# Loading input tiles 10 to 15 later in the DMA queue of a linear-attention and MLP kernel

## The chip, the cores and the metric

The kernel runs on one core of a Trainium2 chip. TensorE (PE) multiplies matrices, VectorE (DVE) and ScalarE (ACT) work element by element and read PE's results from its accumulation banks, GpSimd (POOL) takes part of the same kind of work, and SyncE (SP) issues nearly all DMAs, one after the other. The metric is the time of one execution in microseconds (us); less is better.

## The reference

The input x has 2048 tokens of 512 features. One layer norm is shared by two branches, and the result is x + A(xn) + B(xn):

```python
xn = _layernorm(x)                                   # over the 512 features
# A: linear attention, 32 heads of 16
q, k, v = heads of xn @ wqkv                         # wqkv is 512 x 1536
pq, pk = phi(q), phi(k)                              # phi(t) = (t + 1 if t > 0 else exp(t)) + 1e-6
kv = sum over tokens of pk^T v ; z = sum over tokens of pk
A = (pq @ kv / (pq . z + 1e-6)) @ wo
# B: MLP with a squared relu, 1376 hidden features
B = relu(xn @ w1 + b1)**2 @ w2 + b2
```

The sums kv and z run over all tokens, so they have to be finished before any token's attention can be.

## The kernel before

The 2048 tokens are 16 tiles of 128 (numbered 0 to 15). Float32 products are made of parts: each operand is split into a high part, which PE can take exactly, and the low rest, and three products of parts stand for one.

The program has two halves. The first, up to about 90 us, walks over the tiles and sums `kx`, the products of the keys' features and the normalised tokens. The second, to the end, makes queries, MLP and attention output for four blocks of four tiles. The change lies in the first half.

The program is ordered by hand: every engine executes its instructions in the order in which the Python code issues them, and waits for the inputs of each. SP's queue of DMAs is such an order too: a DMA that has to wait for its source holds up those behind it.

What one tile i passes through in the first half:

- `load_x` (L157) loads raw tokens from DRAM. Tiles 0 to 3 come alone, 4 to 7 in one DMA into `x4`, and 8 to 11 in one DMA into `x8`, each of 1 MB; 12 and 13, and 14 and 15, come in two DMAs of 512 KB each.
- `measure` (L230) takes mean and variance on VectorE (`bn_stats`, `bn_aggr`); `roots` makes the reciprocal root, mainly on POOL; `normalise` (L248) writes the normalised tile `xp`, for tiles from 5 on with ScalarE.
- The tile is needed with the features in the partitions as well. Tiles 0 to 2 are turned by PE. From tile 3 on, `regroup` (L277) stores the tile to DRAM (`via<-xp`, one DMA; for tiles from 6 on one for a pair), `move` (L286) fetches it back in four DMAs (`xg<-via`, `xg4s` for tiles 3 to 5), and `turn` (L291) transposes 32x32 blocks on VectorE. `regroup` puts the moves on a list; `move()` issues what is on it. The moves wait for the store to have landed.
- `transposed` (L314) splits the turned tile into high and low part (ScalarE, then VectorE), and `keep_t` stores the turned tile of the first eight to DRAM for the second half (`xTd<-t`).
- `project` (L373) multiplies with the keys' weights (12 matmuls, `pk`), `phi_k` and `parts` make the features and their parts (ScalarE and VectorE), and `kx` (L390) sums the products with the tokens (12 matmuls).

The loop over steps i from 2 to 15 (L812) starts with `move()`. Then PE does `project(i)` and, at the end of the step, `kx(i - 1)`: 24 matmuls, which take about 5.4 us. In step 3 and later steps up to 10, at the end, the columns of tile i + 2 are turned and split and another `move()` is called (L886 and L887), after which one tile's statistics are measured (L894): tile 10 in step 4, 11 in step 5, 12 in step 6, and so on to 15 in step 9. Tiles 8 and 9 are measured in step 3 (L874).

Before the loop, tile 3 is normalised and stored, and then stand these lines (L645 to L647):

```python
    normalise(*fourth)      # tile 3; its store is issued in here
    load_x(8, x8)
    move()                  # the four moves of tile 3
```

Of the kernel before, what the change touches and what calls it, by code (L numbers as in the profile page):

```python
# [18 lines left out]
def kernel(  # L19
# [59 lines left out]
    def bank(name, tag="ps"):  # L79
        return psum.tile([P, 512], F32, name=name, tag=tag)  # L80
# [6 lines left out]
    def next_tag(of):  # L87
        k, n = turns[of]
        turns[of][0] = (k + 1) % n
        return f"{of}{k}"  # L90

    def two(name):
        return keep.tile([P, 2, 512], F32, name=name, tag=next_tag("x"))

    def four(name, tag, dt=F32, pool=None):
        return (pool or work).tile([P, TB, 512], dt, name=name, tag=tag)
# [60 lines left out]
    def load_x(i, t):  # L157
        n = t.shape[1]
        nc.sync.dma_start(t, xf[i * P:(i + n) * P, :].rearrange("(i p) d -> p i d", i=n))
        for k in range(n):  # L160
            xr[i + k] = t[:, k]
# [11 lines left out]
    def units(f):  # L173


        if f < NF - 1:
            return [(0, f * P, P)]
        return [(0, f * P + Q, 2 * Q), (2 * Q, f * P, Q), (3 * Q, f * P, Q)]
# [10 lines left out]
    def load_o():  # L189
        o = wos[0] = four("wo", "ra")  # L190
        for j in range(NJ):
            cut = P - Q * j
            for a, z, to in ((0, cut, Q * j), (cut, P, 0)):
                if z > a:
                    nc.sync.dma_start(o[to:to + z - a, j], wo[j * P + a:j * P + z, :])
# [34 lines left out]
    def measure(g, *ks):  # L230

        tiles, st, mv, _ = g
        for k in ks or range(len(tiles)):
            nc.vector.bn_stats(st[:, k, :], xr[tiles[k]])  # L234
            nc.vector.bn_aggr(mv[:, k, :], st[:, k, :])
# [6 lines left out]
    def roots(tiles, st, mv, y):  # L242

        n = len(tiles)
        (nc.vector if tiles[0] in (0, 1, 6) else nc.gpsimd).tensor_scalar(y[:, 1, :n], mv[:, :n, 1], 1e-5, None, op0=OP.add)
        nc.gpsimd.tensor_tensor(out=y[:, 0, :n], in0=y[:, 1, :n], in1=power[:, :n], op=OP.pow)

    def normalise(tiles, st, mv, y):  # L248

        n = len(tiles)  # L250
        r, u = (y[:, k, :n] for k in range(2))
        if tiles[-1] >= NACT:

            nc.vector.scalar_tensor_tensor(u, mv[:, :n, 0], -1.0, r, op0=OP.mult, op1=OP.mult)
        later = []

        def last(i, o, src, k):
            nc.scalar.activation(o, src, AF.Identity, bias=u[:, k:k + 1], scale=r[:, k:k + 1])
            if i in groups:
                regroup(i)  # L260

        for k, i in enumerate(tiles):
            o, src = xp[i], xr[i]
            if i >= NDVE:

                o, src = o.rearrange("p g (j c) -> p g j c", j=NJ), gjc(src)
            if i < NACT:
                nc.vector.tensor_scalar(o, src, mv[:, k, 0:1], r[:, k:k + 1], op0=OP.subtract, op1=OP.mult)
                if i in groups:
                    regroup(i)  # L270
            else:
                later.append(lambda a=(i, o, src, k): last(*a))
        return later
# [12 lines left out]
    def move(n=8):  # L286
        for _ in range(n):
            if moves:
                nc.sync.dma_start(*moves.pop(0))
# [22 lines left out]
    def transposed(i, n=1):  # L312

        b, at = i // TB, slot(i)  # L314
        if i < NDVE:
            t = turned_pe(i, n)
        else:
            t = [xT[b][:, :, at] if i >= NPE else w512(f"t{i}", "p", 6).rearrange("p (j t) -> p j t", j=NJ)]
            turn(t[0], xg[i])
        m = NJ // n  # L320
        h, l = ([x[:, k * m:(k + 1) * m, at] for k in range(n)] for x in cols(i))

        def high(k=0):
            nc.scalar.activation(h[k], t[k], AF.Copy)  # L324

        def low(k=0):
            nc.vector.tensor_tensor(out=l[k], in0=t[k], in1=f32(h[k]), op=OP.subtract)

        def keep_t():
            o = t[0]  # L330
            if i < NDVE:
                o = w512(f"t{i}", "p", 6).rearrange("p (j t) -> p j t", j=NJ)
                for k in range(n):
                    copy("act", o[:, k * m:(k + 1) * m], t[k])
            if i < NPE:
                nc.sync.dma_start(xTd[b][:, :, at], o)

        return high, low, keep_t

    def run(*what):  # L340
        for f in what:
            f()
# [30 lines left out]
    def project(i, ps, w, steps, first=True, last=True):  # L373

        for n, (j, u, v) in enumerate(steps):
            nc.tensor.matmul(ps, lhsT=cols(i)[u][:, j, slot(i)], rhs=w[v][:, j, :], start=first and n == 0,  # L376
                             stop=last and n == len(steps) - 1)
# [174 lines left out]
    x4, x8 = four("x4", "r1"), four("x8", "r2")  # L552
    for i0 in range(0, NT, TB):
# [6 lines left out]
        if i0 < NPE:  # L560
            single = work.tile([P, 3, 512], F32, name=f"xg{i0}s", tag="r0")
            for k in range(3):
                i = i0 + k - 1
# [3 lines left out]
        for k in range(0, n, 2):  # L567
            i = i0 + TB - n + k
# [74 lines left out]
    keep1()  # L643
    rests_k("dve", 3)
    normalise(*fourth)  # L645
    load_x(8, x8)
    move()  # L647
    high, low, keep2 = transposed(2)
    high()
# [20 lines left out]
    def tokens_sum(n, tag):  # L670
        return keep.tile([P, 2, 2, 512], F32R, name=f"T{n}", tag=tag)
# [32 lines left out]
    def fetch():  # L704
        while todo and len(held) < 3:
            held.append(todo.pop(0)())
# [95 lines left out]
    def more(i=None):  # L802

        if i is None or i > 12:
            do(extra, counts[0].pop(0))
# [6 lines left out]
    for i in range(2, NT):  # L812
        if i == 13:
            nc.sync.dma_start(b1s[:, :NF - 1], b1[:(NF - 1) * P].rearrange("(f p) -> p f", p=P))
            for a, o, n in units(NF - 1):
                nc.sync.dma_start(b1s[a:a + n, NF - 1:], b1[o:o + n, None])
        move()
        if i in (4, 6):
            load_x(i + 8, two(f"x{i + 8}"))
        if i == 9:  # L820
            load_o()
        if i > 10:
            fetch()
        ps = pks[i] if i < 3 else bank(f"pk{i}")
        if i > 2:
            project(i, ps, wk, HL)
        high = low = keep_t = lambda: None
        if i <= NDVE:
            high, low, keep_t = transposed(i + 1)
        if i == 2:  # L830
            measure(soon)
            roots(*soon)
        later = normalise(*soon) if i == 3 else []

        soon_turned = transposed(i + 2) if 11 <= i and i + 2 < NT else ()

        def mid():
            if i != 3:
                high()
            more(i)  # L840

        def late():
            if i == 3:
                high()
                run(*later)
                tokens(3)
            low()
            more(i)

        if i == 12:  # L850
            rawz = raw_1(NF - 1)
            T.update({n: tokens_sum(n, f"B{n - 1}") for n in (1, 2)})
        if i == 12:
            w = load_1("q", 0)
        if i == 13:
            todo_1 = operands_first(0, w)
            extra.append(todo_1.pop(1))
        if i == 14:
            z = pair("w1z0")
            extra.append(lambda: split(z[:, 0], z[:, 1], rawz, "act", "dve"))  # L860
            o34 = halves(four("Tf", "r0"))
            extra.extend(sums_of(xT[NB - 1], xT[NB - 2], *o34))
            lows = [extra.pop() for k in range(2)]
            extra += [todo_1[0], lows[1], todo_1[1], lows[0], *todo_1[2:]]
        phi_k(i, ps, mid, late)
        more(i)
        run(*soon_turned)
        if i != 3:
            later = normalise(*soon) if soon else []
        if i == 2:  # L870
            ahead[3] = group(6, 7)
            measure(ahead[3], 0)
        if i == 3:
            measure(ahead[4])  # L874
        parts(i)
        if i == 2:
            tokens(2, ahead=False)
            run(*later)
            later = []
        keep_t()  # L880
        if 2 < i < NT - 1:
            tokens(i + 1)
        if i != 3:
            run(*later)
        if NDVE < i + 1 < 12:
            high, low, keep_t = transposed(i + 2)  # L886
            run(high, low, move, keep_t)  # L887
        pieces(int(i > 11))
        if i == 2:
            measure(ahead[3], 1)  # L890
        if i + 2 in (4, 6, 8, 10):
            ahead[i + 2] = group(i + 6, i + 7)
        if 3 < i < 10:
            measure(ahead[(i + 2) // 2 * 2], i % 2)  # L894
        soon = ahead.get(i + 1, ())
        if soon:
            roots(*soon)
        kx(i - 1)
        more(i)
# [66 lines left out]
    for n in range(2):  # L966
# [306 lines left out]
        f = NF - 2  # L1273
# [125 lines left out]
```

## Time and profile before

| | us |
|---|---|
| Time, median of 3 runs | 410.56 |
| lowest and highest run | 410.22 and 410.93 |
| The profiled execution's own time | 410.95 |
| its span in the trace | 409.2 |
| TensorE busy | 402.3 |
| VectorE busy | 308.9 |
| ScalarE busy | 267.6 |
| GpSimd busy | 50.4 |

The span reaches from the first to the last recorded instruction; the rest of the profiled execution's time lies around it. L12 in a row means line 12 of the kernel, and a helper's line stands for all its calls. A row of instructions has its start, its length, the engine, the line, the operation, output and input, and, in brackets, how long the engine had been idle and what ended the idle time. A row of waits has the waiting instruction, what it waited for, and the total, the count and the longest of the waits. A row of windows has, for a stretch of time, its length, the busy time of PE, of PE's weight loads, of VectorE, ScalarE and GpSimd, then the granted clock, the share of the DMA engines in use and the GB/s that they moved.

### The profile page before, as it was taken

To read this page: it belongs to the slowest core of one execution; us is meant where nothing else is said; L and a number is where in the kernel's file an instruction comes from. 1 tells how busy PE (TensorE), PEld (TensorE's weight loads), DVE (VectorE), ACT (ScalarE), POOL (GpSimd) and SP (SyncE) were. 2 spreads that over 40 slices of the span, in tenths; PEclk is the share of its full clock that TensorE was granted. 3 is DMA by queue.
4 is the path that set the end of the run, shared out by engine and by line. 5 is a ranking of instruction groups with operands and counts; after the bars stand their busy time and mean duration, and the time that the engine had idled before them with its cause. 6 is when DMAs were issued, how large, how long until landed. Compare 5 with 4: busy or idle time off the path is not lost.

```text
span 409.2 us, 5634 instructions
## 1 busy us (share of the span) xinstructions
PE 402.3 (98%) x1939; PEld 330.5 (81%) x1939; DVE 308.9 (75%) x560; ACT 267.6 (65%) x465; POOL 50.4 (12%) x81
## 2 busy tenths in 40 slices
PE   8989999999999999999999999999999999999996
PEld 6868888888788888888878888888888888878885
DVE  6877666597898999988349997567989676449833
ACT  4667667556888789887728751677587856837520
POOL 6435333220000000030000300000000200001200
PEclk9999999999999999999999999999999999999999
DMA  6937636820332231272564912411121790034612
GB/s 214 320 121 266 209 104 206 240 45 0 101 109 79 77 103 27 95 198 42 189 229 139 209 34 100 118 53 51 51 79 40 227 197 26 0 108 150 105 26 103
DMA packets 46735, 49.00 MB, mean 120 GB/s; under 512 B 8242, under 2 KB 31026, under 8 KB 46451
## 3 DMA queue, kind: packets, MB, share of 16 engines
q1 hardware_dynamic: 44402, 44.46, 35.1%
q0 software_dynamic: 2304, 4.20, 6.5%
q8 instruction: 15, 0.25, 0.2%
q14 instruction: 14, 0.11, 0.1%
HBM read 37.76 MB, written 9.70 MB: 116 GB/s over the span
## 4 chain that ended last, share of the span: by engine, by line
PE 94%; DMA 2%; DVE 2%; ACT 0%; SPq 0%; issue 0%
PE acc L131 37%; PE b L495 33%; PE kx L396 9%; PE pk L376 9%; PE acc L506 2%; PE pz L131 1%; DMA xg4s<-via 1%; DMA via<-xp 1%; PE b L131 1%; PE pz0b L131 1%; DVE st L234 1%; DMA x<-in_A_x_dram 1%; DVE wkl L581 0%; ACT xs1h L324 0%; PE acc L513 0%; PE pkv L933 0%
## 5 line engine op out<-in xcount | busy, mean ns | idle before, releaser
L131 PE MATMUL acc<-w2r,s 128*128 128x512 f32 x477 | 112.8, 390 | 0.0
L131 PEld LDWEIGHTS acc<-w2r,s 128*128 128x128 f32 x477 | 89.4, 188 | 19.3 <-issue 0.7
L495 PE MATMUL b<-T,aop 128*128 128x512 f32 x336 | 83.4, 389 | 0.0
L495 PEld LDWEIGHTS b<-T,aop 128*128 128x128 f32 x336 | 63.0, 188 | 13.9 <-ACT t L112 0.8
L1071 POOL DMA_DIRECT2D res<-in_B_b_dram x16 | 14.4, 1100 | 276.8 <-DVE dt L437 91.4
L396 PE MATMUL kx<-pk,tok 128*128 128x512 f32 x192 | 46.0, 389 | 0.0
L396 PEld LDWEIGHTS kx<-pk,tok 128*128 128x128 f32 x192 | 36.0, 188 | 7.6
L495 PE MATMUL b<-xs0h,aop 128*128 128x512 f32 x112 | 36.9, 390 | 0.0
L131 PE MATMUL acc<-mh,aTsr 128*128 128x512 f32 x112 | 35.6, 389 | 0.0
L1079 DVE TENSOR_TENSOR res<-acc,res 128x512 f32<-128x512 f32 x16 | 10.7, 689 | 20.4 <-PE acc L131 19.0
L112 ACT ACTIVATE aop<-S 128x512 fp32r<-128x512 f32 x28 | 17.5, 624 | 12.6 <-DVE S L733 12.6
L357 POOL TENSOR_TENSOR tok<-xp,tok 128x512 fp32r<-128x512 f32 x15 | 20.1, 1342 | 39.1 <-ACT tok L112 39.1
L495 PEld LDWEIGHTS b<-xs0h,aop 128*128 128x128 f32 x112 | 21.0, 188 | 4.4
L131 PEld LDWEIGHTS acc<-mh,aTsr 128*128 128x128 f32 x112 | 21.0, 188 | 4.3
L123 DVE TENSOR_TENSOR w2r<-r,w2r 128x512 fp32r<-128x512 f32 (+2 forms) x35 | 23.8, 681 | 0.5 <-ACT w2r L112 0.4
L120 DVE TENSOR_TENSOR aop<-S,aop 128x512 fp32r<-128x512 f32 x28 | 19.2, 687 | 4.8 <-ACT aop L112 4.4
L120 DVE TENSOR_TENSOR s<-c,s 128x512 fp32r<-128x512 f32 x20 | 13.6, 689 | 11.4 <-ACT s L112 11.3
L495 PE MATMUL b<-xs0l,aop 128*128 128x512 f32 x56 | 21.8, 389 | 0.0
L131 PE MATMUL acc<-ml,aTsr 128*128 128x512 f32 x56 | 21.8, 389 | 0.0
L112 ACT ACTIVATE w2r<-r 128x512 fp32r<-128x512 f32 x32 | 19.6, 619 | 2.1 <-DMA out_dram<-res 2.0
L495 PE MATMUL b<-xs1h,aop 128*128 128x512 f32 x56 | 19.5, 389 | 0.0
L112 ACT ACTIVATE T<-Tf 128x512 fp32r<-128x512 f32 x16 | 9.5, 624 | 14.4 <-DVE Tf L676 14.3
(196 smaller groups left out, 751.9 us busy)
## 6 DMA issues: line engine op xcount, KB each, us to landing
r<-in_B_w_dram SPq DMA_DIRECT2D x49, 256.0 KB, 3.1
res<-in_A_x_dram SPq DMA_DIRECT2D x8, 512.0 KB, 4.2
res<-in_B_b_dram POOLq DMA_DIRECT2D x16, 256.0 KB, 5.7
out_dram<-res SPq DMA_DIRECT2D x15, 256.0 KB, 2.1
via<-xp SPq DMA_DIRECT2D x5, 512.0 KB, 2.8
xg<-via SPq DMA_DIRECT2D x20, 128.0 KB, 2.6
x<-in_A_x_dram SPq DMA_DIRECT2D x2, 1024.0 KB, 6.5
xTd<-t SPq DMA_DIRECT2D x8, 256.0 KB, 3.0
```

The source lines that it names most:

```text
L112: nc.scalar.activation(o, i, AF.Copy, bias=bias)
L120: ENG[el].tensor_tensor(out=l, in0=src, in1=f32(h), op=OP.subtract)
L123: nc.vector.tensor_tensor(out=l, in0=src, in1=f32(h), op=OP.subtract)
L131: nc.tensor.matmul(ps, lhsT=a[u], rhs=b[v], start=first and n == 0, stop=last and n == 2)
L234: nc.vector.bn_stats(st[:, k, :], xr[tiles[k]])
L357: ENG[el].tensor_tensor(out=l, in0=src, in1=f32(h), op=OP.subtract)
L376: nc.tensor.matmul(ps, lhsT=cols(i)[u][:, j, slot(i)], rhs=w[v][:, j, :], start=first and n == 0, stop=last and n == len(steps) - 1)
L396: nc.tensor.matmul(kxp[c], lhsT=tok[i][:, u, c * P:(c + 1) * P], rhs=pk[i][:, v], start=i == 0 and (u, v) == first, stop=i == NT - 1 and ( ...
L495: nc.tensor.matmul(ps, lhsT=a[u][:, j * P:(j + 1) * P], rhs=b[v][:, j, :], start=first and j == 0 and n == 0, stop=last and j == 1 and n == 2,
L506: nc.tensor.matmul(ps, lhsT=s[u][:, k * P:(k + 1) * P], rhs=w2s[NF - 1][u][:, a:z], start=first and u == 0, stop=stop and u == 1)
L1071: nc.gpsimd.dma_start(r[:, i], b2[None, :].partition_broadcast(P), accum_op=OP.add)
L1079: nc.vector.tensor_tensor(out=r[:, a:z], in0=ps, in1=r[:, a:z], op=OP.add)
```

## The change

The load of tiles 8 to 11 in front of tile 3's moves becomes a load of tiles 8 and 9 alone, into the first half of the same buffer. Tiles 10 and 11 are loaded into its second half at the start of step 4, where tiles 12 and 13 were loaded; these go to step 5, and tiles 14 and 15 from step 6 to step 7. All loads remain on SP's queue, and the buffers of tiles 12 to 15 are the same.

```diff
@@ -643,7 +643,7 @@
     keep1()
     rests_k("dve", 3)
     normalise(*fourth)
-    load_x(8, x8)
+    load_x(8, x8[:, :2])
     move()
     high, low, keep2 = transposed(2)
     high()
@@ -815,8 +815,10 @@
             for a, o, n in units(NF - 1):
                 nc.sync.dma_start(b1s[a:a + n, NF - 1:], b1[o:o + n, None])
         move()
-        if i in (4, 6):
-            load_x(i + 8, two(f"x{i + 8}"))
+        if i == 4:
+            load_x(10, x8[:, 2:])
+        if i in (5, 7):
+            load_x(i + 7, two(f"x{i + 7}"))
         if i == 9:
             load_o()
         if i > 10:
```

## The prediction

> **What bounds the kernel now.** First the page: the shares of the span and the granted clock.
>
> ```profile
> span 409.2 us, 5634 instructions
> PE 402.3 (98%) x1939; PEld 330.5 (81%) x1939; DVE 308.9 (75%) x560; ACT 267.6 (65%) x465; POOL 50.4 (12%) x81
> PEclk9999999999999999999999999999999999999999
> ```
>
> TensorE (PE) is busy for 402.3 of 409.2 us at full granted clock, so a change can win only from the other 6.9 us. Second, where those lie: the windows, then the waits of PE.
>
> ```profile
> 0.00:24.00 24.00, 20.58 (x97) 16.64 (x98) 16.79 (x37) 12.75 (x25) 11.19 (x29) 1.00 0.77 245
> 24.00:404.00 380.00, 380.00 (x1833) 312.38 (x1832) 290.54 (x522) 254.88 (x440) 39.20 (x53) 1.00 0.39 111
> PE pk L376 <- ACT xs1h L324: 1.8, 2, 1.6
> ```
>
> From 24 to 404 us PE never stops. Before 24 us it stands for 24.00 - 20.58 = 3.42 us, and 1.6 us of that is one wait, on the transposed columns of a token tile. What was late there is in the chain of waits (start, us, what):
>
> ```profile
> 13.05 2.77 DMA via<-xp
> ...
> 15.84 0.33 SPq L289
> ...
> 17.16 4.79 DMA xg4s<-via
> ...
> 21.98 0.72 DVE t L293
> ...
> 22.72 0.64 ACT xs1h L324
> ...
> 23.40 3.02 PE pk L376 x12
> ```
>
> This is tile 3: stored to DRAM, fetched back by four moves, turned by VectorE, split by ScalarE, projected by PE. The last move, 64 KB, took 4.79 us, to 21.95. The DMA issues, looked at in short windows (KB each, us from issue to landing), say how unusual that is; the rows are, in order, the fourth move of tile 3 with its neighbour, two moves of tile 4, the load of tiles 8 to 11, and the loads of tiles 12/13 and 14/15:
>
> ```profile
> xg4s<-via SPq DMA_DIRECT2D x2, 64.0 KB, 4.9
> xg4s<-via SPq DMA_DIRECT2D x2, 64.0 KB, 1.9
> x<-in_A_x_dram SPq DMA_DIRECT2D x1, 1024.0 KB, 7.8
> x<-in_A_x_dram SPq DMA_DIRECT2D x1, 512.0 KB, 5.2
> x<-in_A_x_dram SPq DMA_DIRECT2D x1, 512.0 KB, 4.1
> ```
>
> SP's queue, in order of time:
>
> ```profile
> 13.45 0.43 SPq L159 DMA_DIRECT2D x<-in_A_x_dram  x1
> 15.84 1.76 SPq L289 DMA_DIRECT2D xg4s<-via  x4
> 18.39 0.34 SPq L281 DMA_DIRECT2D via<-xp  x1
> ...
> 33.50 1.73 SPq L289 DMA_DIRECT2D xg<-via  x4
> 35.32 0.52 SPq L336 DMA_DIRECT2D xTd<-t  x1
> 35.89 0.63 SPq L159 DMA_DIRECT2D x<-in_A_x_dram  x1
> 38.51 0.34 SPq L281 DMA_DIRECT2D via<-xp  x1
> 42.41 1.74 SPq L289 DMA_DIRECT2D xg<-via  x4
> 44.24 1.21 SPq L336 DMA_DIRECT2D xTd<-t  x2
> 45.50 0.65 SPq L159 DMA_DIRECT2D x<-in_A_x_dram  x1
> ```
>
> The 1 MB load (13.45) is queued ahead of the moves (15.84) and lands at 13.45 + 7.8 = 21.25; the moves land just behind it, at 21.95. So the load delays tile 3, and with it PE.
>
> **Part 1: half of that load goes.** 512 KB fewer lie ahead of the moves. The soonest that the last move can then land is 17.16 + 1.9 = 19.06. The latest: between 16.0 and 18.4 the queues moved 338 GB/s (the next fence); if the landing moves up only by what 524,288 bytes take at 400 GB/s (an estimate above that rate, so a smaller gain), 1.3 us, it is 20.65. I take a value near the soonest, because by 18.4 us 2.4 x 338 = 811 KB had passed after 16.0, and half a load plus four moves is 524 + 262 = 786 KB: the moves would be through before the next store (18.39) joins.
>
> ```profile
> 16.00:18.40 2.40, 2.40 (x12) 1.99 (x11) 2.23 (x4) 2.13 (x4) 1.70 (x4) 1.00 0.93 338
> 19.17 0.68 DVE L357 TENSOR_TENSOR tok<-xp,tok 128x512 fp32r<-128x512 f32 x1
> 23.40 0.50 PE L376 MATMUL pk<-wkh,xs1h 128*128 128x512 f32 x1 [1.62 <-ACT xs1h L324]
> ```
>
> VectorE works on tile 1's low part until 19.17 + 0.68 = 19.85, so the turn of tile 3 starts at about 19.86 in place of 21.98: **VectorE and ScalarE gain 2.12 us**. PE follows the turn by 23.40 - 21.98 = 1.42 us, so it could start at 21.28; its own earlier matmuls end at 23.40 - 1.62 = 21.78. **PE gains the whole 1.62 us**, and is then bound by itself. At the other bound (20.65) both gain 1.3 us. A loss has no mechanism here: bytes only leave the queue. What is late next, tile 4's turn, hangs on a store at 18.39 that now meets fewer bytes too.
>
> **Part 2: tiles 10 and 11 are loaded in step 4**, where tiles 12 and 13 were: same place in SP's queue (behind the moves of 33.50 and the store of 35.32), same 512 KB. So the 35.89 row prices it: issued at 35.89, landed 5.2 later, 41.09 on the old clock. But tile 10 has a reader in that same step: its statistics on VectorE.
>
> ```profile
> 39.83 0.69 DVE L234 BATCH_NORM_STATS2 st<-x 128x6 f32<-128x512 f32 x1
> 40.55 0.18 DVE L235 BATCH_NORM_AGGREGATE mv<-st 128x2 f32<-128x6 f32 x1
> 40.65 0.66 DVE L371 SCALAR_TENSOR_TENSOR k<-pk,k 128x512 f32<-128x512 f32 x1
> 41.34 0.63 ACT L112 ACTIVATE pk<-k 128x512 fp32r<-128x512 f32 x1 [1.00 <-DVE k L371]
> 42.64 2.88 PE L396 MATMUL kx<-pk,tok 128*128 128x512 f32 x12
> 49.89 0.69 DVE L234 BATCH_NORM_STATS2 st<-x 128x6 f32<-128x512 f32 x1
> 59.95 0.69 DVE L234 BATCH_NORM_STATS2 st<-x 128x6 f32<-128x512 f32 x1
> ```
>
> The statistics start 39.83 - 35.89 = 3.94 us after the issue; the data come after 5.2. **New wait: 1.26 us on VectorE**, whatever the common shift, since the issue hangs on the same chain (tile 5's normalisation, stores, moves) that follows tile 3's turn. Queued behind it on VectorE is the feature map of step 5 (40.65), for it ScalarE's rounding of the keys (41.34), for that the key products on PE (42.64). The rounding ends at 41.97, 0.67 us before PE wants it; with the wait it ends at 43.23. All this is on the old clock. With VectorE's gain it ends at 43.23 - 2.12 = 41.11, while PE, 1.62 earlier, wants it at 41.02: **PE loses about 0.1 us**. In general the net gain is the smaller of 1.62 and VectorE's gain less 0.59. By the bounds of part 1 (2.12 and 1.3) that is 1.53 and 0.71. If the load takes only 4.1 us, as the later one of the same size did, the wait is 0.16 and nothing is lost. ScalarE's further work of that step is also late, but the next key products come 5.4 us later, and VectorE has pauses on the way (1.00 in the 41.34 row).
>
> The Trainium skill, in "DMA: Bandwidth & Descriptors", section "Anatomy of one DMA", fits a transfer as 2.0 us and its bytes at 436 GB/s. By that fit, an estimate, 512 KB take 3.2 us, the data are there before the statistics ask, and part 2 costs nothing. The trace disagrees: 5.2 and 4.1 us for that size, so the rows decide. The same page's "Rules for kernel authors" ask for 1 MiB or more in a DMA, which speaks against cutting the load; by its fit the cut costs another 2.0 us, though only where somebody waits for it.
>
> **Part 3: tiles 12/13 in step 5, 14/15 in step 7.** SP then issues the first between the two stores of the 44.24 row, at 44.24 + 1.21/2 = 44.85, and it lands after 4.1 to 5.2 us, at 48.95 to 50.05; its reader is at 49.89. At worst 0.16 us late, against a slack like the 0.67 above: nothing. The second comes behind the moves of tiles 10 and 11 (issued 51.66 for 1.75):
>
> ```profile
> 51.66 1.75 SPq L289 DMA_DIRECT2D xg<-via  x4
> 58.81 0.34 SPq L281 DMA_DIRECT2D via<-xp  x1
> ```
>
> So it is issued at 53.4 and lands by 58.6, its reader is at 59.95, and the next store at 58.81: nothing. SP issues one DMA more in all, about 0.63 us (35.89 row), ahead of a store of turned columns that only the second half of the program reads: nothing. POOL's queue is not touched.
>
> **Sum.** -1.62 (gap) + 0.1 (new wait on PE) = -1.5 us. The profiled execution took 410.95 us for a span of 409.2; that gives a span near 407.7 and 409.45. It lies 0.39 above the median of 410.56; on the median the forecast is **409.05 us**. No change can be told from a measurement within 0.2%, 0.82 us.
>
> **Rivals.** (a) *The moves gain little.* The bytes that came behind (the store of 18.39) may have shared the engines, so that the landing moves up only by 1.3 us; the net is then 0.71, 409.85. For it: no row shows in which order the engines served the queued bytes. Against: 786 KB fit in before 18.4.
> (b) *No wait at all in step 4*: the load comes within 4.1 us, 1.62 stays, 408.95. For it: the 45.50 row. Against: the 35.89 row is the one at this place, with the same moves before it and the store of 38.51 behind it. The page's fit, above, would give this result.
> (c) *Slower: the load of tiles 10 and 11 is so late that PE stands longer than before.* Place: the key products at 42.64. PE loses there what it won when issue (35.89 - 2.12 = 33.77) + landing + 2.14 (39.83 to 41.97) passes 42.64, which is a landing of 6.7 us; at 7.5 it is 0.8 slower. The 1 MB load took 7.8: with that the time is 33.77 + 7.8 + 2.14 - 42.64 = 1.07 longer, 411.65. Or the issue does not move up, because ScalarE or SP was bound by something else: 35.89 + 5.2 + 2.14 - 42.64 = 0.59 slower. Against: 7.8 is for twice the bytes, and each row between tile 3's turn and the issue is queued behind it.
> (d) *The gap stays* because another input of tile 3's turn is late: 410.55. Against: VectorE is free at 19.85, and the chain of waits puts only the move ahead of the turn.
>
> **Chances.** The forecast 0.62; (a) 0.14, half of it beyond the 0.82 us bound; (b) 0.09; (c) 0.10; (d) 0.05. Faster: 0.62 + 0.09 + 0.07 = 0.78; same: 0.05 + 0.07 = 0.12; slower 0.10. The range goes from (b) less 0.37 us, the reach of the runs from their median, to (a) with the same on top: 408.6 to 410.2. (c) and (d) lie outside. Alone, the forecast's own range is 408.7 to 409.5.
>
> **What would show it.** Right: the moves of tile 3 land before 20 us; PE's wait on the split columns in front of tile 3's projection is under 0.2 us; the load of tile 10 is issued near 33.8 and VectorE's statistics wait on it for about 1.3 us; PE's key products of step 5 wait for ScalarE by 0.1 to 0.3; from then on PE stands nowhere, and its busy time stays 402.3. Wrong: a landing of the moves after 20.7, an issue of tile 10's load near 35.9, a landing over 6 us, or new waits of PE after 60 us, which would mean that the later loads matter.

## The result and the profile after

The changed kernel takes 409.23 us (median; 409.01 to 410.12), the kernel before 410.56 (410.22 to 411.18): a ratio of 0.997, 95% interval 0.9958 to 0.9982, all of it below 1. That is 1.33 us less; 409.05 was forecast. The profiled execution took 410.11 us, with a span of 408.4; among the runs of the changed kernel that is one of the longest, for a reason that lies in its first microseconds and is told below.

The page of the changed kernel (first two lines), its waits of PE and its windows:

```profile
span 408.4 us, 5632 instructions
PE 403.4 (99%) x1939; PEld 331.8 (81%) x1939; DVE 308.4 (76%) x560; ACT 267.7 (66%) x465; POOL 49.8 (12%) x81
...
PE warm L526 <- PEq L1387: 0.8, 1, 0.8
PE pk L376 <- DVE wkh L116: 0.6, 1, 0.6
...
0.00:24.00 24.00, 22.51 (x101) 18.52 (x102) 17.64 (x39) 13.24 (x26) 11.34 (x30) 1.00 0.68 224
24.00:404.00 380.00, 380.00 (x1834) 312.51 (x1833) 289.49 (x520) 254.43 (x440) 38.46 (x51) 1.00 0.40 113
```

PE's wait on tile 3's split columns is gone from the list, and its busy time before 24 us has grown from 20.58 to 22.51 us. The new 0.6 us wait stands at the very start, on the keys' weights. The DMA issues of the weights, looked at in the same short window (2.0 to 2.3 us), first before, then after:

```profile
rk<-in_A_wqkv_dram SPq DMA_DIRECT2D x2, 256.0 KB, 3.8
```

```profile
rk<-in_A_wqkv_dram SPq DMA_DIRECT2D x2, 256.0 KB, 5.4
```

Nothing of the change lies ahead of these loads. They landed 1.6 us later in this execution, and PE's first key products started at 17.11 in place of 16.16. So 1 us of what the change won is hidden in the two profiled executions by an unequal start.

SP's queue, the landing times of the half load, of a move of tile 3 and of the load of tiles 10/11, and VectorE's rows:

```profile
14.63 0.43 SPq L159 DMA_DIRECT2D x<-in_A_x_dram  x1
16.52 1.76 SPq L289 DMA_DIRECT2D xg4s<-via  x4
...
34.74 0.63 SPq L159 DMA_DIRECT2D x<-in_A_x_dram  x1
...
x<-in_A_x_dram SPq DMA_DIRECT2D x1, 512.0 KB, 3.5
xg4s<-via SPq DMA_DIRECT2D x1, 64.0 KB, 1.9
x<-in_A_x_dram SPq DMA_DIRECT2D x1, 512.0 KB, 4.7
...
20.18 0.68 DVE L357 TENSOR_TENSOR tok<-xp,tok 128x512 fp32r<-128x512 f32 x1
20.78 0.70 DVE L293 STREAM_TRANSPOSE t<-xg4s 128x512 f32<-128x512 f32 x1
...
39.51 0.70 DVE L234 BATCH_NORM_STATS2 st<-x 128x6 f32<-128x512 f32 x1 [0.74 <-DMA x<-in_A_x_dram]
```

The last move of tile 3 lands 1.9 us after its issue in place of 4.9; the turn (20.78) follows VectorE's work on tile 1 (20.18) without a wait. In step 4 VectorE stands 0.74 us for tiles 10 and 11. The chain of waits shows what PE makes of it (start, us, what):

```profile
17.27 5.51 PE kx L396 x24
22.78 2.72 PE pk L376 x12
...
39.10 2.72 PE pk L376 x12
41.82 2.92 PE kx L396 x12
44.74 2.72 PE pk L376 x12
```

Twelve matmuls take 2.72 us when nothing disturbs them. Tile 3's projection takes that now, 3.02 before; the key products of tile 5 (the row of 41.82) take 2.92. These are the ones that the prediction and the expectations call the key products of step 5; PE makes them in step 6, between the projections of tiles 6 and 7.

### The profile page after: what moved, and what is told of

Same layout as the page of the kernel before. It is cut to its first block, busy times and chain, and to the rows that moved or that the text cites. A ratio compares the mean times of both kernels' runs of the same rounds, so it can differ in the third digit from the quotient of the medians.

```text
span 408.4 us, 5632 instructions
## 1 busy us (share of the span) xinstructions
PE 403.4 (99%) x1939; PEld 331.8 (81%) x1939; DVE 308.4 (76%) x560; ACT 267.7 (66%) x465; POOL 49.8 (12%) x81
## 4 chain that ended last, share of the span: by engine, by line
PE 97%; DMA 1%; DVE 0%; SPq 0%; issue 0%
PE acc L131 37%; PE b L495 33%; PE pk L376 11%; PE kx L396 11%; PE acc L506 2%; PE pz L131 1%; DMA rk<-in_A_wqkv_dram 1%; PE b L131 1%; PE pz0b L131 1%; PE acc L513 0%; PE pkv L935 0%; PE pm L952 0%; PE pt L308 0%; SPq L159 0%; PE end L131 0%; PE end L506 0%
```

## The experiments

Because starts differ, each profiled execution is read by one account: the start of the first key products (timeline), and the time from there to the projection of step 7 (its start in the chain), less 27.44 us, which is the least that any execution showed for that stretch but for 0.05. The difference is what PE lost in steps 2 to 6. The executions of e7 and e8, in which the granted clock fell, are read apart, further down.

| execution | start | step 7 | loss | its time | time less start and loss |
|---|---|---|---|---|---|
| before | 16.16 | 45.52 | 1.92 | 410.95 | 392.87 |
| changed, first | 17.11 | 44.74 | 0.19 | 410.11 | 392.81 |
| e1, changed | 16.30 | 44.31 | 0.57 | 409.60 | 392.73 |
| e9, changed | 16.43 | 44.16 | 0.29 | 409.48 | 392.76 |
| e2, 1 MB ahead | 16.41 | 45.16 | 1.31 | 410.51 | 392.79 |
| e3, 512 KB before, 512 KB behind the moves | 16.52 | 44.61 | 0.65 | 409.99 | 392.82 |
| e4, all behind the moves | 16.54 | 44.26 | 0.28 | 409.66 | 392.84 |
| e11, 768 KB ahead | 16.43 | 44.27 | 0.40 | 409.59 | 392.76 |
| e6, loads in step 2 | 16.73 | 45.09 | 0.92 | 410.46 | 392.81 |
| e5, late statistics | 16.73 | 44.17 | 0.00 | 409.60 | 392.87 |
| e10, late statistics | 16.51 | 43.90 | -0.05 | 409.27 | 392.81 |

The last column varies by 0.14 us: start and loss account for all differences among these executions, and nothing after step 7 has any part in them.

**The changed kernel again.** No edit.

> The changed kernel once more, as the measure for the other runs of this chip. Theory (bytes): the gap in front of tile 3's projection was the time that the second half of the 1 MB load took ahead of tile 3's moves; it is closed, and VectorE's new wait on the load of tiles 10 and 11 costs PE 0.1 to 0.3 us. Expected: 1.2 to 1.6 us less than before, about 409.1. Rival (later loads): the gain comes from where the loads of tiles 12 to 15 now stand and not from the bytes ahead of tile 3's moves. It expects the same time here; the next two runs tell the two apart.

Measured 409.77 us, ratio to before 0.9971 (0.9961 to 0.9982); 1.30 us less by the medians. Losses of 0.19, 0.57 and, in e9, 0.29 against 1.92.

**Only the rest of the change, the bytes ahead of the moves back.**

```diff
-    load_x(8, x8[:, :2])
+    load_x(8, x8)
     move()
```

> The whole 1 MB load is again ahead of tile 3's moves; all else is as in the changed kernel, so that tiles 10 and 11 are loaded a second time in step 4 and their statistics wait for that. Bytes: the gap of about 1.6 us is back, PE has no lead, and VectorE's wait of 0.7 to 1.3 us exceeds the 0.67 us of slack by 0.1 to 0.6 us: 410.6 to 411.2 us, not faster than before. Later loads: the gain stays, about 409.2 us.

Measured 411.55 us, ratio 1.0019 (1.0004 to 1.0035). Its chain, and then the landing of the second load of tiles 10 and 11:

```profile
17.96 3.62 DMA xg4s<-via
...
23.03 3.06 PE pk L376 x12
...
x<-in_A_x_dram SPq DMA_DIRECT2D x1, 512.0 KB, 4.0
```

The gap is back (a loss of 1.31), with all later loads where the change has them. So the rival, that their places make the gain, falls. The gap is smaller than in the first profile since the last move took 3.62 us and not 4.79; it varies from one execution to the next. In the profiled execution the load of step 4 landed after 4.0 us, just in time, and PE lost nothing there, less than expected. Half of the runs were at 411.9 to 413.7 us, the longest of them at a mean granted clock of 0.996; what PE lost in those was not traced and stays open.

**Only half of the load ahead, all else as early as before** (an edit of the kernel before).

```diff
-    load_x(8, x8)
+    load_x(8, x8[:, :2])
     move()
+    load_x(10, x8[:, 2:])
```

> Only half of the load is ahead of tile 3's moves, the other half (tiles 10 and 11) follows right behind these moves, and tiles 12 to 15 are loaded in steps 4 and 6 as before. Bytes: the gap is closed and nobody waits in step 4: about 409.0 us, 0.1 to 0.3 us under the changed kernel. Tile 4's store has as many bytes ahead of it as before and lands near 22.3 us; its turn may wait by up to 0.3 us, which PE does not feel. Later loads: 410.5 us, as before.

Measured 410.59 us, ratio 0.9992 (0.9983 to 1.0002): not the expected 409.0. Tile 3's gap is closed, but the next fetch pays, in its chain:

```profile
18.78 4.35 DMA via<-xp
...
24.45 1.99 DMA xg4s<-via
...
26.57 0.71 DVE t L293
...
28.00 3.01 PE pk L376 x12
```

Tile 4's store (18.78) now follows the second half and takes 4.35 us, where it took 2.0 us in the changed kernel; its turn and with it the projection of step 4 come late, a loss of 0.65 in all. The bytes had only been passed to the next in the queue. That the change moved tiles 10 and 11 past the store of tile 4 is, by this run, a part of its gain. The runs' median lies 0.6 us above the profiled execution; that rest was not traced.

**Nothing ahead of tile 3's moves.**

```diff
-    load_x(8, x8[:, :2])
     move()
+    load_x(8, x8[:, :2])
```

> As the changed kernel, but the load of tiles 8 and 9 too stands behind tile 3's moves. Bytes, as in the prediction: the moves land as soon as they can, under 2.0 us after the last issue, but VectorE is at work until then and PE is its own bound already, so that the time is that of the changed kernel within 0.3 us. If the half that was left still delayed tile 3, the time falls by over 0.4 us.

Measured 410.16 us, ratio 0.9979 (0.9968 to 0.9989), 0.4 over the changed kernel of the same call. There is no gain, as expected; by the loss (0.28) it is the changed kernel's equal, by the medians 0.1 beyond the expected 0.3. And it shows the same shift as in e3 on a smaller scale: tile 4's turn waits 0.4 us for its moves, and the projection of step 4 takes 2.99.

```profile
DVE t L293 <- DMA xg4s<-via: 0.4, 1, 0.4
...
27.63 2.99 PE pk L376 x12
```

**No wait in step 4.**

```diff
-        if 3 < i < 10:
+        if i == 5:
+            measure(ahead[6])
+        if 5 < i < 10:
             measure(ahead[(i + 2) // 2 * 2], i % 2)
```

> As the changed kernel, but the statistics of tile 10 are taken at the end of step 5, together with those of tile 11, so that no instruction of VectorE in step 4 waits for the load of tiles 10 and 11. Theory (bytes, with a small price for the wait): PE's wait in front of the key products of step 5 is gone, 0.2 to 0.5 us under the changed kernel, 1.5 to 2.1 us under before. Rival (the wait is covered): the statistics waited in PE's slack only, and the time is that of the changed kernel, 1.2 to 1.4 us under before; the two statistics at the end of step 5 then cost as much as they save.

> The changed kernel beside the next two on one chip. From the traces so far, the time of a profiled execution is the start of the first key products on PE, plus what PE loses from there to the projection of step 7 against 27.44 us of pure matmuls, plus 392.8 us. In the changed kernel the loss was 0.2 and 0.6 us, in the kernel before 1.9. Expected: a loss of 0.2 to 0.6 us, 1.2 to 1.6 us under before.

> The changed kernel with the statistics of tile 10 taken in step 5. If its loss is nothing once more, it is 0.2 to 0.6 us under the changed kernel in the same call, and 1.6 to 2.1 us under before. If the earlier difference to the changed kernel came only from the two calls having run on different chips or starts, the two are equal within 0.2 us.

The late statistics measured 409.20 us (0.9958 of before, 0.9945 to 0.9972) and, beside the changed kernel on one chip, 409.13 (0.994, 0.9918 to 0.9962) against 409.57 (0.9951, 0.9931 to 0.997): 0.44 us less by the medians. Against the kernel before it is 2.01 and 1.89 us less by the medians, which agrees with the loss of 1.92 us in the one trace of that kernel. The key products of tile 5 with their neighbours, first in the changed kernel (e9), then with late statistics (e10):

```profile
41.12 0.01 issue
41.13 3.02 PE kx L396 x12
44.16 2.72 PE pk L376 x12
```

```profile
38.46 2.72 PE pk L376 x12
41.18 2.72 PE kx L396 x12
43.90 2.72 PE pk L376 x12
```

So the wait on the load of tiles 10 and 11 does reach PE, and costs 0.2 to 0.6 us in the changed kernel. The late statistics are the fastest version found; PE has no pause left between the first key products and the end.

**The loads of tiles 8 and 9 in step 2** (with late statistics).

```diff
-    load_x(8, x8[:, :2])
     move()
...
         move()
+        if i == 2:
+            load_x(8, x8[:, :2])
```

> As the run before, and the load of tiles 8 and 9 is issued in step 2 behind the moves of tile 4, so that no load lies ahead of the moves of tile 3 or of the store of tile 4. Theory (bytes): neither the projection of tile 3 nor that of tile 4 waits, and nobody waits in step 5: PE runs from its first key products on without a pause, 1.7 to 2.2 us under before. If the load in step 2 delays the store of tile 5 behind it, VectorE's turn of tile 5 waits and some 0.3 us are given back. Rival: the changed kernel has taken what there was, and this is 1.2 to 1.4 us under before.

Measured 410.09 us (0.9974, 0.996 to 0.9988), worse than with the load at its place. What was noted as a risk decides: the store of tile 5 behind the load takes 3.48 us (2.08 in e1), the moves of tiles 6 and 7 are late in turn, and the projection of step 6 is slow to start:

```profile
25.01 3.48 DMA via<-xp
...
34.44 3.25 DMA xg<-via
...
39.31 3.06 PE pk L376 x12
```

**The size between, and two doses beyond.** 768 KB ahead (tile 11 alone in step 4):

```diff
-    load_x(8, x8[:, :2])
+    load_x(8, x8[:, :3])
...
-            load_x(10, x8[:, 2:])
+            load_x(11, x8[:, 3:])
```

> The size between: 768 KB (tiles 8 to 10) ahead of tile 3's moves, tile 11 alone in step 4, tiles 12 to 15 as in the changed kernel; the statistics of tile 10 wait for nothing, those of tile 11 come in step 5. Theory (bytes): 256 KB less than before take 0.8 us off the landing of tile 3's moves, PE's pause of 1.0 to 1.6 us falls to 0.2 to 0.9, the wait of step 4 is gone; the loss is 0.4 to 1.2 us, the time between the two kernels. If the moves land in time already with 768 KB ahead, the loss is nothing and this equals the late statistics.

Measured 409.55 us (0.9956, 0.9938 to 0.9973): a loss of 0.40, at the lower end. The projections of tiles 3 and 4 in its chain:

```profile
22.13 3.02 PE pk L376 x12
...
27.87 2.80 PE pk L376 x12
```

With 512 KB nothing is lost at tile 3, with 768 KB a little (3.02 in place of 2.72), with 1 MB 1.3 to 1.9. Now 512 KB more ahead of the moves than before the change (an edit of the kernel before):

```diff
     load_x(8, x8)
+    load_x(12, two("x12"))
     move()
...
-        if i in (4, 6):
+        if i == 6:
```

> The other direction: as before the change, with the whole 1 MB ahead of tile 3's moves and the 512 KB of tiles 12 and 13 behind it, also ahead of the moves. Theory (bytes): every 512 KB ahead of the moves cost 1.6 us (524 KB at 322 GB/s), PE's gap in front of tile 3's projection grows to 2.8 to 3.3 us, and the time is 1.4 to 1.8 us over before. Rival (it is not the bytes but the order of the later loads): within 0.3 us of before.

Measured 414.10 us (1.0076, 1.0062 to 1.009): 2.9 us longer, twice what was expected. The pause is as expected, 3.02 us, but the matmuls after it are slow. Their rows, the projection in the chain, and the windows (the granted clock is the third number from the end):

```profile
25.23 0.79 PE L376 MATMUL pk<-wkh,xs1h 128*128 128x512 f32 x1 [3.02 <-ACT xs1h L324]
25.82 0.63 PE L376 MATMUL pk<-wkl,xs1h 128*128 128x512 f32 x1
...
25.23 4.47 PE pk L376 x12
...
24.00:25.00 1.00, 0.00 (x0) 0.00 (x0) 1.00 (x2) 0.45 (x1) 0.00 (x0) 0.97 0.07 22
25.00:26.00 1.00, 0.77 (x2) 0.68 (x3) 0.97 (x4) 0.69 (x2) 0.59 (x1) 0.50 0.44 129
27.00:28.00 1.00, 1.00 (x4) 0.71 (x4) 0.97 (x3) 1.00 (x3) 0.24 (x1) 0.50 0.00 0
29.00:30.00 1.00, 1.00 (x7) 0.79 (x6) 0.96 (x3) 0.26 (x1) 0.90 (x2) 1.00 0.71 256
```

The granted clock falls to 0.50 for about 3.4 us, and the projection takes 4.47 in place of 2.72. The loss of 4.76 by the account above holds these 1.75. Last, the wait of step 4 made longer:

```diff
         if i == 4:
+            load_x(12, two("x12"))
             load_x(10, x8[:, 2:])
-        if i in (5, 7):
+        if i == 7:
             load_x(i + 7, two(f"x{i + 7}"))
```

> As the changed kernel, but the load of tiles 12 and 13 is issued in step 4 ahead of that of tiles 10 and 11, which so lands later by the time of another 512 KB, about 1.6 us. By the prediction the net gain is VectorE's lead less the wait beyond the 0.67 us of slack: VectorE waits for 2.2 to 2.9 us, PE loses 1.6 us more than in the changed kernel, and the time is within 0.5 us of before. Rival (the wait is covered by pauses of VectorE and ScalarE): as the changed kernel, 1.2 to 1.4 us under before.

Measured 413.91 us (1.0056, 1.0036 to 1.0076): 2.7 us over before, when the expectation was to be within 0.5 us of it. Its chain and windows:

```profile
34.44 7.02 DMA x<-in_A_x_dram
41.48 0.70 DVE st L234
...
43.69 4.40 PE kx L396 x12
48.09 2.98 PE pk L376 x12
...
44.00:45.00 1.00, 1.00 (x6) 0.80 (x5) 0.98 (x2) 0.16 (x1) 0.77 (x1) 1.00 0.72 233
45.00:46.00 1.00, 1.00 (x4) 0.81 (x3) 0.33 (x1) 0.99 (x2) 0.56 (x2) 0.50 1.03 229
```

The load lands after 7.02 us, VectorE waits 3.6 us, PE pauses 2.82, and the clock halves once more, this time about 1.3 us after PE has resumed: 4.40 in place of 2.72, and 2.98 for the projection behind it. Eight of the ten runs had a mean granted clock of 0.996; the other two, at 0.998 and 1.000, took 410.64 and 412.47 us. The rival that the wait is covered falls.

## Why the prediction held, point by point

- *Tile 3's moves were late because of the load ahead of them*: shown. The move's landing fell from 4.9 to 1.9 us after issue, e2 brings the gap back with nothing else undone, e7 and e11 scale it.
- *The gap is worth 1.62 us*: undersized. That is PE's idle time in the trace; what went was a loss of 1.92 (before) to nothing (e5, e10). Idle is counted from the modelled end of the last matmul, and the first matmuls after a pause are slower (12 in 3.02 us in place of 2.72). On PE's weight loads the same wait lasted 2.04 us.
- *VectorE and ScalarE gain 2.12 us*: near enough. From PE's first key products to tile 3's turn it was 21.98 - 16.16 = 5.82 before and 20.78 - 17.11 = 3.67 after, 2.15 less (1.95 and 2.18 less in e1 and e9).
- *New wait in step 4 of 1.26 us, 0.1 on PE*: here the sizes were off, both ways. The load took 4.7 to 4.9 us in the changed kernel and not 5.2, so VectorE waited 0.74 to 0.84 and not 1.26. But the slack that should have covered it, 0.67, was counted to the first matmul. The weight load ahead of that matmul waited for the rounding too, and where nothing disturbs it, it starts 0.22 us before the matmul (the weight load before the change, then the rounding and the weight load after it):

```profile
42.42 2.68 PEld L396 LDWEIGHTS kx<-pk,tok 128*128 128x128 f32 x12
...
41.03 0.63 ACT L112 ACTIVATE pk<-k 128x512 fp32r<-128x512 f32 x1 [1.84 <-DVE k L371]
...
41.72 2.60 PEld L396 LDWEIGHTS kx<-pk,tok 128*128 128x128 f32 x12 [0.32 <-ACT pk L112]
```

So the slack was 42.42 - 41.97 = 0.45. In the first profile after the change the rounding ends at 41.66, just when the matmul was due (38.94, the start of the projection before it, + 2.72), and 0.22 too late for the weight load; the loss is 0.19. In e1 and e9 it is 0.59 and 0.34 too late, and the losses are 0.57 and 0.29. VectorE's lead over PE, 2.12 - 1.62 = 0.50 in the prediction, was smaller as well, since PE had gained 1.92. So PE lost 0.2 to 0.6, as e5 and e10 show by taking the wait away. The two errors, 0.3 of gain and 0.1 to 0.5 of price, nearly cancel: 1.92 less 0.2 to 0.6 is 1.3 to 1.7, and 1.5 was forecast. The mechanism was right; that the total came so close is in part luck.

- *Tiles 12 to 15 cost nothing*: held. PE waits nowhere after the key products of tile 5, and the last column of the table is the same, within 0.14 us, with the loads in either place. The sign that PE's busy time stays 402.3 did not hold: it is 403.4, and the excess lies ahead of the first key products, which came 0.95 us later.
- *Rival (a), the landing moves up by 1.3 us only*: fell, the moves land at their shortest (1.9 to 2.0 us in the three traces of the changed kernel). *Rival (b), no wait*: fell, VectorE waits in each execution of the changed kernel. The Trainium skill's fit in "DMA: Bandwidth & Descriptors", section "Anatomy of one DMA" (3.2 us for 512 KB, an estimate), is given there for DMAs that GpSimd issues; it agrees with none of the loads of that size that SP issued here with no other load ahead of them, 3.5 to 5.5 us. *Rival (c), too late a load*: not here, but e8 shows the mechanism, at a landing of 7.0 us, and dearer than priced. The prediction's sum gives 0.3 us over before for that landing, and it was 2.7: the price left out the clock, and the load was issued 0.6 us later, behind another. *Rival (d)*: fell.

## What to carry to other kernels

A load that nobody needs soon was not free here: the small fetches queued behind it, which the bound engine waits for, landed after 3.6 to 4.9 us behind 1 MB and after 1.9 to 2.5 us behind 512 KB, so issue such a load behind the small ones. But each place in the queue has somebody behind it and a reader ahead: putting the bytes one place further (e3, e4, e6) passed the delay to the next tile's store. The loads of tiles 8 to 15 stood in SP's queue in all of these runs; whether one issued by another engine would delay the fetches as much was not tried. Move the load and its first reader together, and look at what a pause of TensorE costs by the time from one undisturbed matmul to the next, not by its idle time alone.

## What was not expected of the hardware

- A pause of TensorE of 3.02 us (e7) and one of 2.82 us (e8) were followed by a granted clock of 0.50 for about 3.4 us (24.95 to 28.36 in e7, 45.00 to 48.40 in e8, estimates from the mean clock of short windows). The slower matmuls cost 1.75 us on top in e7 and 1.68 + 0.26 = 1.94 us in e8; the pause of 1.62 us before the change left the clock at 1.00 in the profiled execution. In e8 the clock fell only after PE had worked again for 1.3 us. The Trainium skill, "TensorE: Matmul & The Clock Gate", section "Part 1: The HAM clock gate", has the cold state follow an idle window of about 3.4 us, on windows that run freely. The drop to half and its delay in e8 agree with such windows; the bound does not, as pauses under 3.4 us were enough.
- Of 78 executions of the kernel before that were run beside the experiments, 8 took 412.95 to 414.08 us at a mean granted clock of 0.994 or 0.995, much like those of e7 (0.994 to 0.996). Of 25 executions of the changed kernel none was under 0.998. So the change seems to spare the kernel this as well; none of the 8 was traced, and whether their pause was longer than 1.62 us is not shown.
- The same load of 256 KB of weights at the start landed after 3.7 to 5.4 us (medians of two) in different executions, and the start of the first key products lay between 16.16 and 17.11 us, latest where the weights landed latest, though not in strict order with them. By the table, every microsecond of it is in the kernel's time: it is as large as the effect under study.
